# Fused attention and two MLPs on one core: a set's seventh product is transposed later, and other weights are streamed

## The chip, the cores and the metric

One core of a Trainium2 chip runs the whole program. The metric is the device time of one execution in microseconds (us); lower is better. Three runs of the kernel before gave 1410.61, 1415.06 and 1415.53 us, a median of 1415.06.

## What is computed

Everything is float32. With B = 8 batches, 8 heads, 576 queries of 64 and 32 packed queries `p`:

```python
p_packed = softmax_attention(p, k, v)             # 32 rows per head
x = softmax_attention(q, p_packed, p_packed)      # -> [4608, 512]
g = x @ w_gate
x = (g * sigmoid(g) * (x @ w_val)) @ w_out        # 512 -> 1536 -> 512
h = x @ w_in                                      # 512 -> 2048
out = (h * cos(h)) @ w_out2                       # 2048 -> 512
```

The change lies in the last product, `(h * cos(h)) @ w_out2`, called the down phase of the second MLP here.

## The kernel before

The stages follow one another on the TensorE (PE): attention together with the first MLP's up products, the first MLP's down products, the second MLP's up phase (chunks of rows, eight feature pairs each, `period`), and its down phase, which is the loop at L1265. Every float32 operand is split into a high and a low part (`split`, L115: ScalarE (ACT) copies the high part at L116, VectorE (DVE) subtracts it at L117), and three TensorE passes replace one product.

**The down phase.** The 4608 rows are worked in NCH = 5 sets of 2 x 512 rows (the last two of 2 x 384; `TD`). A set's 2 x 2 x 2 block product is done with seven products instead of eight, in the order ORDER = (0, 4, 6, 1, 2, 3, 5); here they are called the first to the seventh product of a set. One product (`down_mm`, L1062) is 48 matmuls: four pairs of feature blocks `fp`, two blocks in each, two halves `m`, three passes. Its left operand is eight weight tiles `wd[n, f]` of 128 x 512 float32 (256 KB), its right operand four split tiles `g2[n, fp]`, called splits here, which `prep2` (L1102) makes from `raw2`, loaded from the scratch tensor `h2` by `load_g` (L1090). Some `raw2` are first replaced by differences (`sums2`, L1109; the subtraction is L1122). The splits have eight buffers (tile name `xs`, L730), enough for two products.

**What comes out.** `evict2` (L1138) is called after a product. After the first, fourth, fifth and sixth product ACT copies the accumulators (L1032) into `part` tiles; after the second, fifth and sixth DVE adds (L1035). `finish_out` (L1124) writes one quarter of a set's output: two DVE transposes (L1128) into a tile `ot`, then four stores (L1133) of 128 KB (96 KB in the small sets). They are queued on POOL (GpSimd), in the last set on SP and ACT. `ot` has two buffers (L1126), so a `finish_out` waits for the four stores of the last but one. The second product finishes one quarter, the sixth finishes two, one behind the other, and the seventh finishes one: its transposes read the accumulators `pb` and `pd` in PSUM directly.

**The weights.** All 56 weight tiles of a set would be needed again in every set. 43 slots of 256 KB exist (`U_AREAS`, L48), handed out in the order in which they were given back (`ut`, L925, `ut_done`, L929). Eight are kept for `part` tiles. Three products' tiles stay for good (24 slots); the four products in `RING` (L51) are streamed, 11 tiles ahead: when a streamed product has been issued, its eight tiles are given back and eight loads (`load_wd`, L960) are issued on SP. The first 35 loads (`wd_first`, L954) are issued late in the up phase, as its weights are given back.

**The order of the work** is written by hand and is the program's order on each engine. For a set `s_` and place `i` it is: the product; `sums2` and the splits of the next product (splits first at the second and fifth product); `load_g` of the next set's rows (at the fifth, sixth and seventh product); the eight weight loads; `evict2`. So SP issues row loads, weight loads and, in the last set, stores in one queue, and DVE meets the seventh product's transposes after the splits of the next set's first product and ahead of those of its second:

```python
                for fp in range(4):
                    if s_ + i:
                        prep2(*nxt2(s_, i), fp)
```

Of the kernel before, what the change touches and what calls it, by code (L numbers as in the profile page):

```python
# [33 lines left out]
NCH = len(TW)  # L34
T0 = tuple(2 * sum(TW[:c]) for c in range(NCH))
D0 = tuple(2 * sum(TD[:c]) for c in range(NCH))
NPF = NF2 // 2
# [10 lines left out]
U_AREAS = (6, 4, 4, 6, 6, 6, 2, 4, 4, 1)  # L48
U_FIRST = (0, 7, 4, 5, 2, 8, 9, 3, 6, 1)
QS = 5  # L50
RING = (4, 1, 3, 5)  # L51
ATT1 = (7, 10, 10, 11, 13, 13, 14, 15, 15, 18, 18, 19, 20)
VISIT1 = (17, 18)
FIRST2 = (14, 14, 14, 16)
# [17 lines left out]
def attention_mlp_kernel(ctx: ExitStack, tc: tile.TileContext, qT, kT, vP, pP, wgv, w12, out):  # L72
# [665 lines left out]
    with tc.manual_schedule():  # L738
# [186 lines left out]
        def ut(key, shape, dt, name):  # L925
            tag_of[key] = free_u.pop(0)
            return lt(shape, dt, "u%d" % tag_of[key], name, U_AREAS[tag_of[key]])

        def ut_done(key):  # L929
            free_u.append(tag_of.pop(key))  # L930
# [20 lines left out]

        wd = {}
        wd_ring = [(n, f) for n in RING for f in range(NPF)] * NCH
        wd_first = [(n, f) for n in (0, 4, 6, 1, 2) for f in range(NPF) if n not in RING]  # L954
        ahead = sum(U_AREAS) - 8 - len(wd_first)
        for k, (n, f) in enumerate(wd_ring[:ahead]):
            wd_first.insert((8 if n == 4 else 16) + k, (n, f))
        del wd_ring[:ahead]

        def load_wd():  # L960
            n, f = (wd_first or wd_ring).pop(0)
            wd[n, f] = ut(("wd", n, f), [128, 2, 256], F32R, "wd")
            SP.dma_start(out=wd[n, f].bitcast(F32).rearrange("p x c -> p (x c)"), in_=w2d[f, PIECE[n]])
# [67 lines left out]
        def copy(out, in_):  # L1031
            ACT.activation(out=out, in_=in_, func=AF.Copy)  # L1032

        def plus(out, x, y):
            DVE.tensor_tensor(out=out, in0=x, in1=y, op=ALU.add)  # L1035
# [26 lines left out]
        def down_mm(s_, i, fps, ms_all=((0, 1),)):  # L1062
            n, w = ORDER[i], TD[s_]
            which = {0: 0, 1: 0, 3: 0, 4: 1, 6: 2, 2: 3, 5: 3}[n]
            first = n in (0, 4, 6, 2)
            if first and 0 in fps:
                if which == 3:
                    acc2[which] = [x[:, :w] for x in bd_tiles()]
                else:
                    o2 = ac_tile("o2")  # L1070
                    acc2[which] = [o2[:, m, :w] for m in range(2)]
            acc = acc2[which]
            for ms in ms_all:
                for fp in fps:
                    for j in range(2):
                        for m in ms:
                            for q, (x, y) in enumerate(PASSES):
                                PE.matmul(  # L1078
                                    out=acc[m], lhsT=wd[n, 2 * fp + j][:, x, 128 * m:128 * m + 128],
                                    rhs=g2[n, fp][:, y, j, :],  # L1080
                                    start=(first and fp + j + q == 0), stop=(fp, j, q) == (3, 1, 2),
                                    skip_group_check=not first,
                                )
            for fp in fps:
                del g2[n, fp]
            return acc
# [3 lines left out]
        def load_g(s_, k, t):  # L1090
            if s_ < NCH:
                w = TD[s_]
                r0 = D0[s_] + w * t
                for fp in range(4):
                    r = raw2[s_, k, t, fp] = xt("raw2", w)
                    f0 = NPF * k + 2 * fp
                    SP.dma_start(out=r, in_=h2[f0:f0 + 2, :, r0:r0 + w].rearrange("f p n -> p f n"))
# [4 lines left out]
        def prep2(s_, n, fp):  # L1102
            if s_ >= NCH:
                return
            r = raw2[(s_, *QUAD[n], fp)]
            g = g2[n, fp] = new_xs(TD[s_])
            split(r, g[:, 0], g[:, 1])

        def sums2(s_, i):  # L1109
            todo = {  # L1110
                1: [((0, 1), (0, 1), (0, 0), fp) for fp in range(4)],
                2: [((1, 1), (1, 1), (0, 1), fp) for fp in range(4)],
                3: [((0, 0), (1, 1), (0, 0), fp) for fp in range(4)],
                4: [((1, 0), (1, 0), (1, 1), fp) for fp in (0, 1)],
                5: [((1, 0), (1, 0), (1, 1), fp) for fp in (2, 3)],
            }
            if s_ == 0:
                todo[1] = [x[fp] for fp in range(4) for x in (todo[1], todo[2])]
                todo[2] = []
            for to, x, y, fp in todo.get(i, ()):  # L1120
                to, x, y = (raw2[(s_, *kt_, fp)] for kt_ in (to, x, y))
                DVE.tensor_tensor(out=to, in0=x, in1=y, op=ALU.subtract)  # L1122

        def finish_out(s_, a, t, o_):  # L1124
            w = TD[s_]
            ot = lt([128, w // 32, 2, 32], F32, "v", "ot", 2)  # L1126
            for m in range(2):
                DVE.transpose(out=ot[:, :, m, :], in_=o_[m])  # L1128
            r0 = D0[s_] + w * t
            queues = (nc.gpsimd,) if s_ < NCH - 1 else (SP, ACT) if (a, t) == (1, 0) else (SP,)  # L1130
            for al in range(4):
                c0 = 128 * al + 64 * a
                queues[al % len(queues)].dma_start(  # L1133
                    out=out[r0:r0 + w, c0:c0 + 64].rearrange("(b r) d -> r b d", r=32),
                    in_=ot[32 * al:32 * al + 32].rearrange("p b m c -> p b (m c)"),
                )

        def evict2(s_, n, acc):  # L1138
            for m in range(2):
                if n in (0, 1, 2, 3):  # L1140
                    part2[n, m] = ut((n, m), [128, TX], F32, "part")[:, :TD[s_]]
                    copy(part2[n, m], acc[m])

            def pop(k):
                for m in range(2):
                    ut_done((k, m))
                return [part2.pop((k, m)) for m in range(2)]

            def add(o_, x, y):
                for m in range(2):  # L1150
                    plus(o_[m], x[m], y[m])

            if n == 2:
                add(acc, pop(1), acc)
            elif n == 4:
                o_ = pop(0)
                add(o_, o_, acc)
                finish_out(s_, 0, 0, o_)
            elif n == 3:
                w_, c22 = pop(3), pop(2)  # L1160
                add(c22, w_, c22)
                finish_out(s_, 1, 1, c22)
                add(w_, w_, acc2[2])
                finish_out(s_, 0, 1, w_)
            elif n == 5:
                finish_out(s_, 1, 0, acc)
# [95 lines left out]
        def nxt2(s_, i):  # L1262
            return (s_, ORDER[i + 1]) if i < 6 else (s_ + 1, ORDER[0])

        for s_ in range(NCH):  # L1265
            for i in range(7):
                n = ORDER[i]
                acc = down_mm(
                    s_, i, (2, 3) if s_ == i == 0 else range(4), ((0,), (1,)) if (s_, i) == (NCH - 1, 6) else ((0, 1),)
                )  # L1270
                if i not in (1, 4):
                    sums2(s_, i)
# [3 lines that stand above are left out]
                if i in (1, 4):  # L1276
                    sums2(s_, i)
                if i == 4:
                    load_g(s_ + 1, 0, 0)
                elif i == 5:  # L1280
                    load_g(s_ + 1, 1, 1)
                    load_g(s_ + 1, 0, 1)
                elif i == 6:
                    load_g(s_ + 1, 1, 0)
                if n in RING:
                    for f in range(NPF):
                        del wd[n, f]
                        ut_done(("wd", n, f))
                        if wd_ring:
                            load_wd()  # L1290
                if s_ or i != 1:
                    if s_ == 0 and i == 2:
                        evict2(s_, *early)
                    evict2(s_, n, acc)
                else:
                    early = n, acc
# [41 lines left out]
```

## Time and profile before

| | us |
|---|---|
| median of three runs (lowest, highest) | 1415.06 (1410.61, 1415.53) |
| the profiled execution | 1411.97 |
| its span, first to last instruction | 1410.2 |
| PE busy in it | 1384.7 |
| VectorE busy | 1121.2 |
| ScalarE busy | 817.6 |
| POOL busy | 239.1 |

The profile is of one execution; its times run from its first instruction. A wait is the idle time of an engine in front of an instruction, with what ended it. PEclk is the granted TensorE clock as a share of its full speed. The down phase takes about the last 365 us of the span.

### The profile page before, as it was taken

The page shows a single profiled execution, that of the slowest core. Times are in us where ns is not written, and L with a number is a line of the kernel's source. Part 1 is how long each engine was busy: PE and PEld are TensorE (multiplying, and loading weights), DVE is VectorE, ACT ScalarE, POOL GpSimd, SP SyncE. Part 2 cuts the span into 40 slices and gives each one's busy share as a digit, 9 for nine tenths or more (in the row PEclk, how much of TensorE's full clock was granted, in tenths as well). Part 3 has the DMA queues.
Part 4 walks back from the last instruction along what each step waited for, and adds up shares of the span by engine and source line. Part 5 has one row for each costly group of instructions (what it writes and reads, how often), then busy time and mean ns, then how long its engine had stood idle before and what let it go on. Part 6 is the DMA issues. An engine that isn't in the chain of part 4 may idle for free.

```text
span 1410.2 us, 23890 instructions
## 1 busy us (share of the span) xinstructions
PE 1384.7 (98%) x8972; PEld 1193.9 (85%) x8972; DVE 1121.2 (80%) x1396; ACT 817.6 (58%) x1119; POOL 239.1 (17%) x392
## 2 busy tenths in 40 slices
PE   8999999999999999999999999999999989999998
PEld 6678888888898888898888999888888878788998
DVE  5779889889866898988857787878679677685876
ACT  5866566666644556554557787768674425253433
POOL 1112222222231111121011111111110010111120
PEclk9999999999999999999999999999999999999999
DMA  8947978877698648458467584748977947657773
GB/s 318 402 178 275 352 260 309 310 283 287 247 410 312 230 163 297 147 193 303 163 263 243 194 290 184 277 147 301 399 273 255 372 129 274 235 178 271 237 269 93
DMA packets 161043, 363.87 MB, mean 258 GB/s; under 512 B 22944, under 2 KB 37792, under 8 KB 159520
## 3 DMA queue, kind: packets, MB, share of 16 engines
q1 hardware_dynamic: 123808, 236.56, 48.5%
q0 software_dynamic: 35456, 123.76, 22.4%
q10 hardware_dynamic: 1664, 2.03, 0.4%
q8 instruction: 71, 1.16, 0.3%
q14 instruction: 44, 0.36, 0.1%
HBM read 236.98 MB, written 125.30 MB: 257 GB/s over the span
## 4 chain that ended last, share of the span: by engine, by line
PE 80%; DMA 7%; issue 6%; DVE 5%; ACT 1%; POOL 1%; SPq 0%; DVEq 0%; POOLq 0%; ACTq 0%
PE o L657 17%; PE ac L992 14%; PE o L1078 13%; PE pv L540 7%; PE pd L992 7%; PE pg L540 7%; PE pb L992 3%; PE wp L500 3%; PE pb L1078 2%; PE pd L1078 2%; PE pv L529 2%; DMA wd<-w2d 1%; PE pg L529 1%; DMA w2u<-w2p 1%; DMA out<-ot 1%
## 5 line engine op out<-in xcount | busy, mean ns | idle before, releaser
L1078 PE MATMUL o<-xs,wd 128*128 128x512 f32 (+1 forms) x1200 | 253.5, 372 | 8.9 <-DVE xs L117 8.9
L657 PE MATMUL o<-g,w 128*128 128x512 f32 (+1 forms) x1260 | 259.7, 368 | 1.4 <-DVE g L117 1.4
L1078 PEld LDWEIGHTS o<-xs,wd 128*128 128x128 f32 x1200 | 221.5, 190 | 39.1 <-DVE xs L117 10.4
L657 PEld LDWEIGHTS o<-g,w 128*128 128x128 f32 x1260 | 219.3, 189 | 41.5 <-DVE g L117 1.9
L992 PE MATMUL ac<-xs,up 128*128 128x512 f32 (+1 forms) x960 | 210.8, 367 | 0.7 <-ACT v L1032 0.7
L992 PEld LDWEIGHTS ac<-xs,up 128*128 128x128 f32 x960 | 175.1, 188 | 23.6 <-ACT v L1032 1.1
L116 ACT ACTIVATE xs<-raw 128x1024 fp32r<-128x1024 f32 (+1 forms) x140 | 130.5, 973 | 98.2 <-DVE raw L1122 77.9
L117 DVE TENSOR_TENSOR xs<-raw,xs 128x1024 fp32r<-128x1024 f32 (+1 forms) x140 | 146.9, 1110 | 12.3 <-ACT xs L116 12.3
L540 PE MATMUL pv<-a,wp 128*128 128x288 f32 x1008 | 150.6, 298 | 3.0 <-DVE h L572 2.8
L540 PEld LDWEIGHTS pg<-a,wp 128*128 128x128 f32 x1008 | 137.7, 188 | 16.8 <-issue 5.7
L116 ACT ACTIVATE g<-hr 128x1024 fp32r<-128x1024 f32 (+1 forms) x105 | 101.3, 976 | 85.7 <-DVE hr L637 35.1
L540 PE MATMUL pg<-a,wp 128*128 128x288 f32 x1008 | 150.3, 298 | 0.4 <-ACT E L213 0.4
L540 PEld LDWEIGHTS pv<-a,wp 128*128 128x128 f32 x1008 | 137.6, 188 | 11.5 <-DVE h L572 5.7
L117 DVE TENSOR_TENSOR g<-hr,g 128x1024 fp32r<-128x1024 f32 (+1 forms) x105 | 113.1, 1114 | 30.0 <-ACT g L116 29.9
L558 ACT ACTIVATE silu<-pg 128x576 f32<-128x576 f32 x96 | 62.5, 652 | 112.7 <-PE pg L540 103.9
L572 DVE TENSOR_TENSOR h<-silu,pv 128x576 f32<-128x576 f32 x96 | 72.1, 751 | 52.2 <-PE pv L540 18.2
L992 PE MATMUL pd<-xs,up 128*128 128x512 f32 (+1 forms) x480 | 111.7, 367 | 0.0
L992 PEld LDWEIGHTS pd<-xs,up 128*128 128x128 f32 x480 | 87.7, 188 | 11.5
L573 POOL DMA_DIRECT2D h<-h x96 | 53.4, 557 | 244.6 <-DVE h L572 222.9
L1133 POOL DMA_DIRECT2D out<-ot x64 | 41.5, 648 | 261.0 <-issue 128.8
L1122 DVE TENSOR_TENSOR raw<-raw,raw 128x1024 f32<-128x1024 f32 (+1 forms) x80 | 84.5, 1109 | 0.1
L1021 DVE SCALAR_TENSOR_TENSOR cp<-ac,cp 128x1024 f32<-128x1024 f32 (+1 forms) x40 | 44.7, 1117 | 46.4 <-ACT cp L1018 42.6
(132 smaller groups left out, 2005.4 us busy)
## 6 DMA issues: line engine op xcount, KB each, us to landing
wd<-w2d SPq DMA_DIRECT2D x184, 256.0 KB, 5.5
up<-w2u SPq DMA_DIRECT2D x140, 256.0 KB, 4.2
h<-h POOLq DMA_DIRECT2D x96, 288.0 KB, 5.4
hr<-h SPq DMA_DIRECT2D x48, 512.0 KB, 7.0
raw<-h SPq DMA_DIRECT2D x48, 512.0 KB, 5.6
raw<-in_w SPq DMA_DIRECT2D x44, 512.0 KB, 4.9
w2u<-w2p POOLq DMA_DIRECT2D x24, 512.0 KB, 4.9
w2d<-w2p POOLq DMA_DIRECT2D x24, 512.0 KB, 5.8
```

Of the source, the lines that this page charges most:

```text
L116: ACT.activation(out=hi, in_=src, func=AF.Copy)
L117: eng.tensor_tensor(out=lo, in0=src, in1=hi.bitcast(F32), op=ALU.subtract)
L500: PE.matmul(out=p_[cols(c), r, :], lhsT=pp_of(b, r, c), rhs=wg[m][rows(r), c // 2, c % 2].rearrange("p a n -> p (a n)"), start=True, stop= ...
L540: PE.matmul(out=p_[:, c, :HS], lhsT=w[:, u, x, o:o + 128], rhs=a2[b][:, u, y, HS * c:HS * c + HS], start=(n == 0), stop=(n == 5),)
L558: ACT.activation(out=s_, in_=pg[:, :, :HS], func=AF.Silu)
L572: DVE.tensor_tensor(out=h_, in0=s_, in1=pv[:, :, :HS], op=ALU.mult)
L573: nc.gpsimd.dma_start(out=h1[f, :, S * b:S * b + S], in_=h_.rearrange("p c n -> p (c n)"))
L657: PE.matmul(out=acc[:, m, :N], lhsT=wd1[n, fp][:, j, 256 * x + 128 * m:256 * x + 128 * m + 128], rhs=g1[n, fp][:, y, j, :], start=(first a ...
L992: PE.matmul(out=out, lhsT=w[:, u, 128 * k:128 * k + 128], rhs=x[:, v, k, :], start=(first and k == 0 and i == 0), stop=(k == 1 and i == 2) ...
L1021: DVE.scalar_tensor_tensor(out=out, in0=h_, scalar=1.0 / TWO_PI, in1=out.bitcast(I32), op0=ALU.mult, op1=ALU.subtract)
L1078: PE.matmul(out=acc[m], lhsT=wd[n, 2 * fp + j][:, x, 128 * m:128 * m + 128], rhs=g2[n, fp][:, y, j, :], start=(first and fp + j + q == 0), ...
L1122: DVE.tensor_tensor(out=to, in0=x, in1=y, op=ALU.subtract)
```

## The change

The streamed products become those at the second to fifth place (numbers 4, 6, 1, 2); the tiles of the first, sixth and seventh (0, 3, 5) stay. The first 35 loads are the eight of product 0, eleven of the ring (eight of 4, three of 6), then those of 3 and 5. And for all sets but the last, `evict2` of the seventh product is called in the next set, after the splits of that set's second product have been issued and just before `evict2` of its first product.

```diff
-RING = (4, 1, 3, 5)
+RING = (4, 6, 1, 2)
...
         wd_ring = [(n, f) for n in RING for f in range(NPF)] * NCH
-        wd_first = [(n, f) for n in (0, 4, 6, 1, 2) for f in range(NPF) if n not in RING]
-        ahead = sum(U_AREAS) - 8 - len(wd_first)
-        for k, (n, f) in enumerate(wd_ring[:ahead]):
-            wd_first.insert((8 if n == 4 else 16) + k, (n, f))
+        ahead = sum(U_AREAS) - 8 - 8 * (7 - len(RING))
+        wd_first = [(0, f) for f in range(NPF)] + wd_ring[:ahead] + [(n, f) for n in (3, 5) for f in range(NPF)]
         del wd_ring[:ahead]
...
                         if wd_ring:
                             load_wd()
-                if s_ or i != 1:
+                if i == 0 and s_:
+                    evict2(*last)
+                if i == 6 and s_ + 1 < NCH:
+                    last = s_, n, acc
+                elif s_ or i != 1:
                     if s_ == 0 and i == 2:
                         evict2(s_, *early)
                     evict2(s_, n, acc)
```

## Rows read from the trace of the kernel before

**Rows 1.** The page, busy time by engine: us, share of the span, instructions.

```profile
PE 1384.7 (98%) x8972; PEld 1193.9 (85%) x8972; DVE 1121.2 (80%) x1396; ACT 817.6 (58%) x1119; POOL 239.1 (17%) x392
```

**Rows 2.** Waits of PE, whole span: who, for whom, us in total, times, longest.

```profile
PE o L1078 <- DVE xs L117: 8.9, 4, 3.9
```

**Rows 3.** Timeline of PE at four set boundaries: start, us, what [idle before, releaser].

```profile
1137.64 2.93 PE L1078 MATMUL o<-xs,wd 128*128 128x512 f32 x6 [3.88 <-DVE xs L117]
...
1217.98 2.37 PE L1078 MATMUL o<-xs,wd 128*128 128x512 f32 x9 [1.50 <-DVE xs L117]
...
1294.95 2.45 PE L1078 MATMUL o<-xs,wd 128*128 128x384 f32 x10 [3.06 <-DVE xs L117]
...
1355.53 2.72 PE L1078 MATMUL o<-xs,wd 128*128 128x384 f32 x14 [0.50 <-DVE xs L117]
```

**Rows 4.** Timeline of DVE at the first boundary.

```profile
1117.26 4.59 DVE L117 TENSOR_TENSOR xs<-raw,xs 128x1024 fp32r<-128x1024 f32 x4
1135.17 0.72 DVE L1128 STREAM_TRANSPOSE ot<-pb 128x512 f32<-128x512 f32 x1 [13.32 <-DMA out<-ot]
...
1136.40 9.13 DVE L117 TENSOR_TENSOR xs<-raw,xs 128x1024 fp32r<-128x1024 f32 x8
```

**Rows 5.** Waits of DVE from 1060 to 1410 us.

```profile
DVE ot L1128 <- DMA out<-ot: 44.9, 5, 13.3
```

**Rows 6.** Timeline of POOL at the first boundary: first and last of eight stores.

```profile
1115.35 0.65 POOL L1133 DMA_DIRECT2D out<-ot  x1 [21.54 <-DVE ot L1128]
...
1143.84 0.66 POOL L1133 DMA_DIRECT2D out<-ot  x1 [2.48 <-issue]
```

**Rows 7.** The out stores issued on POOL from 1115 to 1127 us, three.

```profile
DMA to landing us min/median/max: 5.2/5.4/5.8
```

**Rows 8.** The out stores issued on POOL from 1132 to 1138.1 us, three.

```profile
DMA to landing us min/median/max: 2.4/2.4/2.4
```

**Rows 9.** Stretches: engines' busy us, then PEclk, DMA share, GB/s.

```profile
1117.00:1127.00 10.00, 10.00 (x45) 8.28 (x45) 4.85 (x5) 4.25 (x4) 0.71 (x2) 1.00 1.05 402
1127.00:1135.00 8.00, 6.76 (x30) 5.26 (x28) 0.00 (x0) 1.43 (x3) 1.26 (x2) 1.00 0.42 151
```

**Rows 10.** Stretches behind two of the waits (PEclk is third from the end).

```profile
1137.60:1141.00 3.40, 3.36 (x8) 2.69 (x9) 3.40 (x4) 0.84 (x1) 0.96 (x2) 0.50 0.16 41
...
1295.00:1298.00 3.00, 3.00 (x13) 3.00 (x14) 3.00 (x4) 0.55 (x1) 0.66 (x1) 0.72 0.38 93
```

**Rows 11.** Chain that ended last, pieces: start us, us, what.

```profile
1059.87 30.15 PE o L1078 x133
...
1137.64 35.09 PE o L1078 x143
...
1217.98 32.75 PE o L1078 x143
...
1294.95 26.63 PE o L1078 x143
...
1355.53 25.08 PE o L1078 x143
```

**Rows 12.** Timeline of ACT at the first boundary: first product evicted.

```profile
1133.57 1.09 ACT L1032 ACTIVATE part<-o 128x512 f32<-128x512 f32 x2 [9.82 <-PE o L1078]
```

**Rows 13.** The POOL store issued at 1143.84 us alone.

```profile
DMA to landing us min/median/max: 3.7/3.7/3.7
```

**Rows 14.** Timeline of POOL, third boundary: the eighth store after the sixth product.

```profile
1301.56 0.66 POOL L1133 DMA_DIRECT2D out<-ot  x1 [2.57 <-issue]
```

**Rows 15.** Timeline of SP: first set's last row loads, first ring loads; last set's ring loads.

```profile
1042.60 25.00 SPq L1097 DMA_DIRECT2D raw<-h  x8
1067.69 14.99 SPq L963 DMA_DIRECT2D wd<-w2d  x16
...
1369.00 15.08 SPq L963 DMA_DIRECT2D wd<-w2d  x13
```

**Rows 16.** The weight load issued at 1067.69 us alone.

```profile
DMA to landing us min/median/max: 4.5/4.5/4.5
```

## The prediction, made before the changed kernel ran

> **What bounds the kernel now.** The page comes first: PE is busy 98% of the span [rows 1], so only PE's idle time, or time at a lower clock, can be won. PE's waits: the down phase has one kind, 8.9 us in four, each for a split that DVE writes [rows 2]. Its timeline shows where: in front of the second product of the second to fifth set, 3.88, 1.50, 3.06 and 0.50 us [rows 3], together 8.94.
>
> Why are those splits late? At the first boundary DVE finishes the first product's splits near 1121.9, idles 13.32 us until a store has landed, does the two transposes of the old set's seventh product, then eight splits without a pause [rows 4]: their inputs had long been ready, they only stood behind the transposes. Such waits for stores sum to 44.9 us in five [rows 5]. The transposes need one of two `ot` buffers, so the four stores of the sixth product's first quarter must have landed. POOL issues its stores one after another, the next when the last has landed: 1115.35 is the first, 1143.84 the eighth [rows 6]. The first three took 5.4 us each [rows 7], the next three 2.4 [rows 8]. The DMA share was 1.05 in the first stretch and 0.42 in the second [rows 9].
>
> Two of the waits cost more than their length. After 3.88 us of idling PE runs at the lower of its two levels (granted clock 0.50, so 1.2 instead of 2.4 GHz), and after 3.06 us part of the stretch does (0.72) [rows 10]. The chain prices it: the 143 matmuls that follow (three products) take 35.09 us after the 3.88 us wait and 32.75 after the 1.50 us wait, so 2.34 more; in the small sets 26.63 against 25.08, so 1.55 more [rows 11]. A product thus takes 10.92 us (32.75 / 3), or 8.36 (25.08 / 3).
>
> **The change part by part.** *Transposes moved, four sets.* Eight DVE transposes and sixteen POOL stores go behind the second product's splits. Removed from PE's path: 8.94 + 2.34 + 1.55 = 12.83 us. No instruction is added. On ACT nothing is queued behind them, and POOL has no other work there, so its order stays. `pb` and `pd` stay full until the next set's first product; they are written again only at its fifth, some four products later.
>
> Behind the transposes on DVE now stand the third product's splits. ACT can't copy for these before it has evicted the first product, at 1133.57 [rows 12]; the transposes came free at 1135.17 [rows 4]. The third product would start two products after the first ends, or about 1133.8 + 10.9 = 1144.7, and needs one split of 1.14 us (9.13 / 8). So this place has some 8 us to spare and costs nothing.
>
> *What is late next.* The second product's quarter takes the next `ot` buffer, and so needs the eighth store. If DVE waits there, it holds four subtractions (priced as splits, 4.6 us) and the fourth product's splits. The first product ends at 1137.64 - 3.88 = 1133.76, the fourth starts two products later, at 1155.6; less 1.4 for the transposes (2 x 0.72), 4.6 and 1.14, the eighth store may land as late as 1148.5. It landed at 1143.84 + 3.7 = 1147.5 [rows 6, 13]: 1.0 to spare even at the old pace. At the third boundary, where a small set follows a large one, the first product ends at 1294.95 - 3.06 = 1291.9 and the fourth starts at 1308.6; with the pieces at three quarters (5.4 us together), the limit is 1303.2, and the store of 1301.56 would land at about 1305.3 [rows 14, 13]: 2.1 us late at the old pace, nothing once the stores go 0.3 us each faster.
>
> *Streamed weights.* As many loads as before: 35 first, then 149, 256 KB each. What moves is when. In the old order the sixth and seventh product give back sixteen slots, so weight loads run just when the stores start. In the new one no weight slot comes free between the fifth product and the next set's second; of the eight loads issued after that second product, six have slots free earlier and go with the row loads, the rest wait for PE. So most of the 1.05 share of [rows 9] should be gone and the stores be nearer 2.4 than 5.4 us. By itself this gives the sum nothing; it removes the 2.1. The last row loads of a set no longer stand behind eight weight loads on SP, which only helps.
>
> The price: four streamed products in a row. In steady state each tile is issued over a product ahead of its use, against some 5 us of landing, so nothing shows. Two places are tight. In the first set, tiles four to eight of the third product are issued only after the row loads, which hold SP until about 1067.6; the first ring load goes at 1067.69 [rows 15] and lands 4.5 us later [rows 16], at 1072.2. The fourth product ends at 1059.87 + 30.15 = 1090.0 [rows 11], so the third starts near 1068.2 and wants that tile after 18 of 48 matmuls, at 1072.3. Bounds: 0 late at 4.5 us; 1.2 at the 5.8 us of the slowest loaded store [rows 7]. I take 0.2, since the same queue with the same row loads ahead gave 4.5. In the last set the second product's four stores stand on SP ahead of the fourth product's tiles; ring loads went at 1369.00 [rows 15], 5.1 us after that product's end (1355.53 + 8.36), and the tile is wanted 11.5 us after it (1.375 products): with 4.5 to 5.8 us of landing it has 0.6 to 1.9 to spare.
>
> The Trainium skill has a rule against half of this. SBUF — State Buffer (the "DVE blocks DMA" trap) says that DVE work in certain modes keeps GpSimd from writing the descriptors of its DMAs. By it, moving weight loads would not quicken the stores, and the 2.1 us would stay. The trace speaks against it: DVE did nothing from 1121.9 to 1135.2 [rows 4], and the third store, issued inside that stretch (1115.35 plus two landings), still took over 5 us [rows 6, 7].
>
> *Sum.* 12.83 - 0.2 = 12.6 us; 1411.97 - 12.6 = 1399.4 for the profiled execution, which was 3.1 below the median of the three runs and 1.4 above their lowest. Taken off the median it is 1402.5. I predict between the two, 1401.0.
>
> **The rivals.** *Part of the wait comes back* (0.16). The stores keep their pace, 2.1 us return at the third boundary with up to 1.55 of slow clock, and the first set's tiles are 1.2 late, perhaps with 2.34 of slow clock: at most 7.2 back, so 1403 to 1408. Of this chance 0.06 is for the stores' pace alone, 2.1 to 3.7 us back, 1403.1 to 1404.7. (By the Trainium skill's rule above, that part would come.) For it: both margins are near zero. Against: less DMA traffic at the boundary.
>
> *Nothing gained* (0.08). The second splits would be late for another reason, or the wait reappears whole one product later; about 1414. Against: eight splits without a pause [rows 4], and 8 us to spare behind the transposes.
>
> *Slower* (0.04). The wait for `ot` moves to the second product's quarter and is larger there, since DVE then holds subtractions and splits. With x us from store to store, the eighth lands 8x after the first: in the trace x = (1147.5 - 1115.35) / 8 = 4.0 [rows 6, 13]. The limit there is 1148.5 - 1115.35 = 33.2 us, so from x = 4.15 on each large boundary stalls 8x - 33.2. At x = 5.4, the loaded landing, that is 10.0 us at each of three, with 2.34 of slow clock behind each: 37 lost against 12.8 won, some 1439. It needs the streamed loads, now four products in a row, to fall into the stores. Against: they begin only with the second product.
>
> **How the numbers follow.** A measurement of this kernel can tell about 0.5%, or 7.1 us. The forecast, all four waits and both slow stretches gone, has 0.72: 1397 to 1404 with the spread of the runs shown. The range runs from 1396 to 1407: below, the lowest run less the sum is 1398, with a little for runs whose waits were longer than the profile's; above, it takes in most of the first rival. Faster by over 0.5% is below 1408.0: the forecast and nearly all of the first rival, 0.86. Within 0.5%: 0.10. Slower: 0.04.
>
> **What would show it.** Right: PE's waits for DVE in the down phase under 1 us; no stretch below PEclk 1.00 there but at the end; 143 matmuls behind a boundary in 32.8 (25.1) us; at a boundary DVE does eight splits, then the transposes; the stores after the sixth product land in under 4 us from the second or third on. Wrong: a wait of PE at the fourth product of a set behind `ot` (the slower rival); a wait of PE for a weight load in the first set's third product; a wait of the second splits that remains.

## The result, and the profile after

The changed kernel takes 1398.17 us in the median of four runs (1396.23 to 1401.20), the kernel before 1412.84 in its four; the ratio is 0.9898, with a 95% interval of 0.9868 to 0.9929. The prediction was 1401.0, between 1396 and 1407. The profiled execution took 1396.23 us, with a span of 1394.4.

On the page of the changed kernel (busy us, share and instructions by engine, then the costliest group of the down phase with its idle time at the end), the idle time in front of the down phase's matmuls is gone ([rows 1], [rows 2]).

```profile
PE 1378.6 (99%) x8972; PEld 1190.4 (85%) x8972; DVE 1121.7 (80%) x1396; ACT 817.6 (59%) x1119; POOL 239.1 (17%) x392
...
L1076 PE MATMUL o<-xs,wd 128*128 128x512 f32 (+1 forms) x1200 | 248.4, 367 | 0.0
```

The timelines of DVE and of POOL at the first boundary of the changed kernel (start, us, what, idle before it and releaser):

```profile
1115.57 9.13 DVE L117 TENSOR_TENSOR xs<-raw,xs 128x1024 fp32r<-128x1024 f32 x8
1127.21 0.72 DVE L1126 STREAM_TRANSPOSE ot<-pb 128x512 f32<-128x512 f32 x1 [2.51 <-DMA out<-ot]
...
1133.96 4.63 DVE L117 TENSOR_TENSOR xs<-raw,xs 128x1024 fp32r<-128x1024 f32 x4 [5.43 <-ACT xs L116]
```

```profile
1113.67 0.65 POOL L1131 DMA_DIRECT2D out<-ot  x1 [16.08 <-DVE ot L1126]
1119.00 0.66 POOL L1131 DMA_DIRECT2D out<-ot  x1 [4.68 <-issue]
...
1135.55 0.66 POOL L1131 DMA_DIRECT2D out<-ot  x1 [2.16 <-issue]
```

Against [rows 4], the eight splits of two products now run in one piece ahead of the transposes, and DVE waits 2.51 us for the stores instead of 13.32. Against [rows 6], the eighth store is issued 21.9 us after the first (1135.55 - 1113.67) instead of 28.5. The stretches of [rows 9], at the same times, show why (PEclk, DMA share and GB/s at the end), and so do the six stores after the first, issue to landing:

```profile
1117.00:1127.00 10.00, 10.00 (x46) 8.29 (x45) 7.70 (x7) 2.13 (x2) 1.97 (x3) 1.00 0.45 149
1127.00:1135.00 8.00, 8.00 (x37) 6.64 (x36) 2.36 (x3) 3.11 (x5) 1.97 (x3) 1.00 0.25 65
```

```profile
DMA to landing us min/median/max: 2.4/2.4/2.8
```

The DMA share fell from 1.05 to 0.45 (to 0.57 from 1115.3 to 1125.3 us, which is as far behind the first store as the stretch of [rows 9] was). What SP issued there before (start, us, what):

```profile
1110.95 2.39 SPq L1097 DMA_DIRECT2D raw<-h  x4
1113.63 11.88 SPq L963 DMA_DIRECT2D wd<-w2d  x14
```

Now SP issues four weight loads there, from 1115.1 to 1116.6 us, and nothing else from 1110 to 1133. The first store, beside those four, still took 5.0 us. The chain of the changed kernel has no break at a boundary any more; the first four products of a set are one piece each (192 matmuls):

```profile
1120.97 43.52 PE o L1076 x192
...
1197.13 43.52 PE o L1076 x192
...
1273.29 33.30 PE o L1076 x192
...
1331.56 33.28 PE o L1076 x192
```

Three quarters of 43.52 are 32.64, and of 33.28 they are 24.96: the pace that [rows 11] shows behind the short waits, without the 35.09 and 26.63 behind the long ones.

### The profile page after: what moved, and what is told of

The parts are those of the page before. It is cut to its first block, busy times and chain, and to the rows that moved or that the text cites. A ratio compares the mean times of both kernels' runs of the same rounds, so it can differ in the third digit from the quotient of the medians.

```text
span 1394.4 us, 23883 instructions
## 1 busy us (share of the span) xinstructions
PE 1378.6 (99%) x8972; PEld 1190.4 (85%) x8972; DVE 1121.7 (80%) x1396; ACT 817.6 (59%) x1119; POOL 239.1 (17%) x392
## 4 chain that ended last, share of the span: by engine, by line
PE 89%; DVE 4%; DMA 3%; issue 2%; ACT 1%; POOL 0%; ACTq 0%; POOLq 0%; SPq 0%; DVEq 0%
PE o L1076 18%; PE o L657 17%; PE ac L990 14%; PE pd L990 7%; PE pv L540 7%; PE pg L540 7%; PE pb L990 4%; PE pd L1076 4%; PE pb L1076 4%; PE wp L500 2%; PE pv L529 2%; PE pg L529 1%; DMA qt<-in_qT 1%; DMA hr<-h 1%; PE tp L229 1%
## 5 line engine op out<-in xcount | busy, mean ns | idle before, releaser
L1076 PE MATMUL o<-xs,wd 128*128 128x512 f32 (+1 forms) x1200 | 248.4, 367 | 0.0
L1076 PEld LDWEIGHTS o<-xs,wd 128*128 128x128 f32 x1200 | 218.5, 188 | 28.1
L1120 DVE TENSOR_TENSOR raw<-raw,raw 128x1024 f32<-128x1024 f32 (+1 forms) x80 | 84.5, 1110 | 0.1
```

The costliest lines, as they stand in the source:

```text
L1076: PE.matmul(out=acc[m], lhsT=wd[n, 2 * fp + j][:, x, 128 * m:128 * m + 128], rhs=g2[n, fp][:, y, j, :], start=(first and fp + j + q == 0), ...
```

## The experiments

Each kernel was timed beside the kernel before on the same chip. The first two make one half of the change each.

**The transposes moved, the weights as before.** The edit is the second half of the diff alone:

```diff
+                if i == 0 and s_:
+                    evict2(*last)
+                if i == 6 and s_ + 1 < NCH:
+                    last = s_, n, acc
+                elif s_ or i != 1:
```

> Only the transposes of the seventh product are moved; the streamed weights are those of before. Theory (the splits were late only because they stood behind the transposes): the four waits of 8.9 us and the slow clock of 3.9 us go even though the stores keep their old pace, 5 to 6 us for the first two or three at a boundary; about 2 us come back as a wait of PE at the fourth product of the fourth set, where the eighth store lands too late for the second product's quarter. Ratio to before 0.991 to 0.993. Rival (the stores' pace is what counts, the order on DVE only shifts the wait): PE's waits for DVE in the down phase stay over 5 us in total, at the third or fourth product, and the ratio is over 0.995.

Measured: ratio 0.9938 (0.9916 to 0.9959). PE's waits in the down phase, then the first three stores at the first boundary, issue to landing:

```profile
PE o L1078 <- DVE xs L117: 2.1, 1, 2.1
PE o L1078 <- ACT xs L116: 1.2, 1, 1.2
```

```profile
DMA to landing us min/median/max: 5.2/5.2/5.3
```

The timeline of DVE at the third boundary shows the place, the second product's quarter:

```profile
1295.12 1.01 DVE L1035 TENSOR_TENSOR part<-part,o 128x384 f32<-128x384 f32 x2
1300.65 1.04 DVE L1128 STREAM_TRANSPOSE ot<-part 128x384 f32<-128x384 f32 x2 [4.52 <-DMA out<-ot]
1301.61 3.52 DVE L1122 TENSOR_TENSOR raw<-raw,raw 128x768 f32<-128x768 f32 x4
1305.05 1.82 DVE L117 TENSOR_TENSOR xs<-raw,xs 128x768 fp32r<-128x768 f32 x2
```

The four waits are gone though the stores are as slow as in [rows 7], and a wait comes back where the limit of the prediction placed it, behind the `ot` buffer of the second product's quarter at the third boundary: 1.2 and 2.1 us in front of the fourth product's first matmuls, 3.3 where about 2 was expected. The rival, that the wait would only shift, is out; the ratio came a little above the expected range, as the 1.2 us and the slow clock behind the wait came on top.

**The weights changed, the transposes as before.** The edit is `RING` and `wd_first` of the diff.

> Only the streamed weights are changed; the transposes stay ahead of the second product's splits. Theory: weight loads no longer run beside the first stores, so after the first one or two a store lands in 2.4 us, the fourth about 13 us after the first was issued instead of 20. The transposes then run some 4 us before the first product ends, the second splits are ready in time, and the waits are under 1 us in total, the clock never drops: ratio 0.990 to 0.993, so that either part alone wins nearly all and the two do not add. Rival (GpSimd's stores are held up by something else than the weight loads, DVE's work for instance): first stores of 5 us as before, waits of 8.9 us as before, ratio 0.998 to 1.002.

Measured: ratio 0.9907 (0.9885 to 0.9929), with no wait of PE for DVE in the down phase. DVE at the first boundary:

```profile
1117.60 4.59 DVE L117 TENSOR_TENSOR xs<-raw,xs 128x1024 fp32r<-128x1024 f32 x4
1128.67 0.72 DVE L1126 STREAM_TRANSPOSE ot<-pb 128x512 f32<-128x512 f32 x1 [6.48 <-DMA out<-ot]
...
1129.91 4.59 DVE L117 TENSOR_TENSOR xs<-raw,xs 128x1024 fp32r<-128x1024 f32 x4
```

DVE still waits in front of the transposes, but 6.48 us instead of 13.32. The first product, 10.9 us from 1123.0, ends at 1133.9; the second splits start 4 us ahead of that. The chain from the start of the first set's fifth product to the start of the last transpose:

```profile
1090.36 0.68 PE pb L1076 x3
...
1391.87 0.58 DVE ot L1126
```

That is 301.51 us, and the changed kernel's chain takes the same 301.51 there (its two lines are shown below). So this half alone wins all that the whole wins, and the halves do not add: each takes away the same waits. The weight loads and the row loads both run earlier in this kernel; which of them counts for how much was not tried.

**The changed kernel again**, beside these.

> The changed kernel unaltered, beside the others on one chip. Both theories: ratio 0.987 to 0.993 as measured before; no wait of PE for DVE in the down phase. It gives the difference of each part to the whole on the same chip.

Measured: ratio 0.9900 (0.9880 to 0.9919), 1399.41 us. PE waited for DVE nowhere in the down phase. The difference to the kernel with the weights alone is inside the intervals.

**The waits filled with matmuls**, in the kernel before:

```diff
+                if s_ and i == 1:
+                    hold = ac_tile("hold")
+                    for _ in range((0, 14, 5, 10, 0)[s_]):
+                        PE.matmul(
+                            out=hold[:, 0], lhsT=wd[0, 0][:, 0, :128], rhs=wd[0, 0].rearrange("p x c -> p (x c)"),
+                            start=True, stop=True,
+                        )
```

> The kernel before, with 14, 5 and 10 additional matmuls into an unused accumulator ahead of the second product of the second, third and fourth set, which fill 3.2, 1.1 and 2.3 us of the waits and compute nothing that is used. Theory (the slow stretch comes from PE's idling): the granted clock stays at full level, the three products behind the first and third wait take 32.8 and 25.1 us instead of 35.1 and 26.6, and 2 to 4 us are saved: ratio 0.997 to 0.9985. Rival (the stretch is slow because DVE delivers splits late behind the transposes): these times stay as they were, or the kernel gets slower, ratio 0.9995 or more.

Measured: ratio 0.9975 (0.9962 to 0.9988). PE at the first boundary, and the chain's pieces behind the four:

```profile
1131.68 3.34 PE L1271 MATMUL hold<-wd 128*128 128x512 f32 x14
1134.85 5.38 PE L1078 MATMUL o<-xs,wd 128*128 128x512 f32 x21
```

```profile
1135.37 32.75 PE o L1078 x143
...
1214.94 32.75 PE o L1078 x143
...
1292.72 25.09 PE o L1078 x143
...
1351.66 25.06 PE o L1078 x143
```

The splits come no earlier than before and the waits are filled in part (PE still idled 1.95 and 1.57 us at the second and third boundary), and 35.09 and 26.63 us became 32.75 and 25.09. PE's idling is what slowed it; that term, 3.9 us by [rows 11], is 3.5 by the ratio (0.0025 of 1412.55), with 1.7 to 5.4 inside the interval.

**The third product's weight tiles earlier in the first set.** In the second profiled execution of the changed kernel PE waited 0.9 us for a weight load there, in the first it had not. So here five tiles are loaded ahead of the last four row loads:

```diff
         load_g(0, 1, 1)
+        for _ in range(5):
+            load_wd()
         load_g(0, 0, 1)
...
-                        if wd_ring:
+                        if wd_ring and (s_, i) != (0, 1) or f > 4 and wd_ring:
```

> The changed kernel, but in the first set the third product's last five weight tiles are loaded ahead of the last four row loads, not after them. Theory (PE waits there in some executions for the fourth tile: the weight load after 1070.25 us came 1.55 us late-to-next in the second look at the changed kernel, against a usual 0.23): no gap there, the chain no longer passes through a weight load or a store of the up phase, 0 to 1.3 us saved against the changed kernel, ratio to before 0.987 to 0.992. Rival (the row loads, now 2.4 us later on SP, become the late ones): a wait of PE for splits in the first set, and the kernel 1 to 4 us slower than the changed one.

> The changed kernel unaltered, beside the others: ratio 0.988 to 0.992; a gap of up to 1.6 us between weight loads near 1070 us, or none.

Measured: 1397.45 us, ratio 0.9895 (0.9873 to 0.9918), against 1400.01 and 0.9911 (0.9891 to 0.9930) for the changed kernel. In the latter's profile PE waited in front of the third product's fourth tile (waits of PE, then its timeline):

```profile
PE o L1076 <- DMA wd<-w2d: 1.4, 1, 1.4
```

```profile
1069.83 3.56 PE L1076 MATMUL o<-xs,wd 128*128 128x512 f32 x15
1074.79 5.51 PE L1076 MATMUL o<-xs,wd 128*128 128x512 f32 x23 [1.40 <-DMA wd<-w2d]
```

In the former it waited for nothing in the down phase. To tell whether it is the faster kernel, both were timed again:

> The kernel with the five early tiles a second time, to tell whether it beats the changed one by more than the spread. Theory (a wait of 1 to 2 us in most executions of the changed kernel goes): median 1 to 2 us below the changed kernel's in the same sitting, no gap between weight loads over 0.35 us in the down phase. Rival (the 2.6 us between the two medians of the sitting before were spread): medians within 1 us of each other, either way.

> The changed kernel unaltered beside it: ratio to before 0.988 to 0.992; in the first set a wait of PE for a weight load of 0 to 1.5 us.

Measured: 1398.82 (0.9905, 0.9885 to 0.9925) and 1399.00 us (0.9909, 0.9890 to 0.9928). Again the wait was 1.4 us in the changed kernel and absent in the other, but the medians now lie 0.2 us apart, so most of the 2.6 us between those of the first pair was spread. The wait is gone in both profiled executions with early tiles, its 1.4 us are less than these runs can tell, and no version is shown to beat the changed kernel.

**Slower stores.** The four stores of the sixth product's first quarter are issued twice in the first four sets, once in the changed kernel and once with the transposes left where they were:

```diff
-            for al in range(4):
+            for al in range(4) if s_ == NCH - 1 or (a, t) != (1, 1) else (0, 0, 1, 1, 2, 2, 3, 3):
```

> The changed kernel with the four stores of the sixth product's first quarter issued twice (the same data), in the first four sets. So the first ot buffer comes free after eight stores and the second after twelve. Theory of the limit (the second quarter's last store may land 33.2 us after the first was issued at a large boundary, about 27 at the third): no wait at the second or third product; 2 to 4 us of wait at the fourth product after the first two boundaries, 8 to 12 after the third, ratio to before 1.000 to 1.006. Rival (nothing on PE waits for stores once the transposes are moved): ratio 0.990 to 0.994.

> The same doubled stores, with the new streamed weights but the transposes left ahead of the second product's splits. Theory (here the limit is nearer: the first quarter's stores must land before the first product ends, about 17 us after the first was issued): 7 to 10 us of wait at the second product of the second, third and fourth set each, with a slow clock behind each, ratio to before 1.008 to 1.018, so the move is worth 8 to 20 us where stores are slower, though next to nothing where they are not. Rival (the move is worth nothing in any case): the same time as with the transposes moved, within 3 us.

Measured: 1431.47 us with the transposes moved, ratio 1.0150 (1.0119 to 1.0180), and 1439.77 without, 1.0196 (1.0174 to 1.0219). So the move is worth 8.3 us here (every run with it is faster than every run without), at the low end of what was expected, and both are slower than expected. PE's waits, moved and not moved:

```profile
PE o L1076 <- DVE xs L117: 13.5, 6, 3.5
PE o L1076 <- ACT xs L116: 7.0, 4, 2.1
```

```profile
PE o L1076 <- DVE xs L117: 32.9, 4, 9.7
```

The expectation for the unmoved one left out the fourth boundary, which waited like the others (7.97 us). For the moved one, "no wait at the second or third product" failed: the third product waited 0.38 us at the first boundary and 3.51 at the third. With the fourth product's waits that makes 5.1, 4.9, 7.7 and 2.8 us at the four boundaries, where 2 to 4, 2 to 4, 8 to 12 and none were expected, and the clock was lower behind each of them (0.50 to 0.72). The first boundary on DVE shows what the limit had missed:

```profile
1141.65 0.72 DVE L1126 STREAM_TRANSPOSE ot<-pb 128x512 f32<-128x512 f32 x1 [16.16 <-issue]
...
1142.89 4.59 DVE L117 TENSOR_TENSOR xs<-raw,xs 128x1024 fp32r<-128x1024 f32 x4
1147.40 4.62 DVE L1120 TENSOR_TENSOR raw<-raw,raw 128x1024 f32<-128x1024 f32 x4
1151.94 1.28 DVE L1033 TENSOR_TENSOR part<-part,o 128x512 f32<-128x512 f32 x2
1153.60 1.31 DVE L1126 STREAM_TRANSPOSE ot<-part 128x512 f32<-128x512 f32 x2 [0.38 <-DMA out<-ot]
1154.83 4.59 DVE L1120 TENSOR_TENSOR raw<-raw,raw 128x1024 f32<-128x1024 f32 x4
1159.34 4.62 DVE L117 TENSOR_TENSOR xs<-raw,xs 128x1024 fp32r<-128x1024 f32 x4
```

The second quarter's store, which the limit was about, held DVE only 0.38 us. It was the seventh product's transposes, late by their own stores, that pushed a row of work almost without gaps: from 1141.65 to the fourth product's splits at 1159.34 it is 17.7 us. (The profile names no releaser for the transposes' 16.16 us; the last of the eight stores ahead of them was issued on POOL at 1137.77 and landed 3.6 us later, at 1141.4.)

## Why the prediction was right, and where its terms were off

**The waits.** That the splits were late only for their place in DVE's queue is shown by the kernel with the move alone: slow stores, and the four waits gone. The term was 8.94 us, and it was too small. From the start of the first set's fifth product to the start of the last transpose, the chain of the kernel before and that of the changed one give

```profile
1090.02 0.68 PE pb L1078 x3
...
1405.62 0.58 DVE ot L1128
```

```profile
1088.33 0.68 PE pb L1076 x3
...
1389.84 0.58 DVE ot L1126
```

315.60 and 301.51 us, 14.1 saved where 12.83 were summed. (The other 1.7 us between the profiled executions lie ahead of that point, where the change moves nothing but the order of some weight loads. In the attention PE waited 1.4 us for a load of `qt` in the profile of before and not in that of the changed kernel; nothing here ties that to the change.) The page of before has a better measure of the waits than [rows 2], the idle time in front of PE's weight loads (last on the line, with its releaser):

```profile
L1078 PEld LDWEIGHTS o<-xs,wd 128*128 128x128 f32 x1200 | 221.5, 190 | 39.1 <-DVE xs L117 10.4
```

10.4 + 3.89 = 14.3, within 0.2 of the 14.1. So PE's idle time tells each of the four waits some 0.37 us too short. One part of that is seen: a matmul's end in the trace is modelled, and a 128x512 matmul is recorded with 394 ns where 227 pass from one to the next (43.52 / 192), so its end lies some 0.17 us behind the point from which the next could have run. The rest is not explained.

**The slow clock.** 3.89 us by the chain. With the waits filled the two pieces shortened by 3.88, and the kernel by 3.5 (1.7 to 5.4). Right.

**The streamed weights.** "By itself this gives the sum nothing" failed. The prediction counted the waits to the move and the 2.1 us at the third boundary to the weights. The mechanism was right, stores of 2.4 us once the weight loads are gone; but the transposes' start under quick stores was not worked out, and it alone clears the second splits with 4 us to spare. In the changed kernel the first transpose starts at 1127.21, ahead of the first product's end near 1131.9, so there the move has nothing left to take. The sum is the same, since both halves take the same waits, and that the number came out although the prediction gave the waits to one half alone is luck. The move alone takes 306.95 us where the whole takes 301.51 (chain, as above): 5.4 short, with the late eighth store at the third boundary that was forecast as 2.1 and measured 3.3 and the lower clock behind it.

On the stores' pace, the Trainium skill's trap in SBUF — State Buffer (the "DVE blocks DMA" trap), that DVE work in certain modes keeps GpSimd from writing descriptors, names copies as such work. That the subtractions and transposes which DVE does here are of that kind was assumed when the prediction made a rival of it, and no run shows it: the stores were quick with the new weights. The trace of before also shows two stores of 2.4 us while DVE was busy throughout (issue to landing of the two, then the stretch; DVE busy is the third number after the length):

```profile
DMA to landing us min/median/max: 2.4/2.4/2.4
```

```profile
1164.00:1169.40 5.40, 5.40 (x26) 4.46 (x25) 5.40 (x6) 3.95 (x4) 1.31 (x2) 1.00 0.25 53
```

**The price of four streamed products in a row.** Bounds of 0 to 1.2 us, 0.2 taken. Four profiled executions of the changed kernel show 0, 0.9, 1.4 and 1.4: the place was right, the size too small, and the upper bound as well. So one of the prediction's signs of being wrong, a wait of PE for a weight load there, did appear, in three of four profiles. It is paid once, and is less than the spread of the runs.

**The spare room behind the transposes.** "Some 8 us to spare" looked only at the next product, and left out the two transposes themselves: they take 1.2 us ([rows 4]: 1135.17 to 1136.40), so it was 7. (The third product starts one product after the first ends, as that sum has it, not two as the sentence says.) The slower stores show that 17.7 us of DVE work, and a split of 1.2, stand between the transposes' start and the fourth product, which begins two products (21.8 us) after the first ends: so they may start about 3 us after that end, not 8. In the kernel before they came free 1.4 us after it ([rows 3], [rows 4]); with the move alone nothing was lost there, so the size did not matter to the result.

**The rivals.** Nothing gained and slower are out, and of the first rival only the late tiles came. The slower rival's place, the second product's quarter, exists (2.1 us with the move alone), but with slower stores the transposes themselves were the first to be late.

## What to carry to other kernels

When an engine with a fixed order of work waits for a transfer, look first at what stands behind the waiting instruction: moving it behind work whose inputs are ready removes the wait without making the transfer faster. Then ask what slows the transfer; if one cure is enough, the two do not add (here the new weights alone won everything, the move alone all but 5.4 us), and the second buys room for worse days (8.3 us with doubled stores) rather than time. Judge that room by all the work queued on the engine up to the next deadline it can miss, not by the next item.

## What the runs showed of the hardware

POOL's stores of 128 KB landed in 2.4 to 2.8 us in stretches with a DMA share of 0.25 to 0.45, and in 5.2 to 5.8 us when issued beside weight and row loads at a share near 1, so there the stores, one in flight at a time, lose more than half their pace. Weight loads alone do it: in the kernel before, the third store, issued at 1126.95, took 5.4 us, though the last row load, issued at 1113.0, had landed 8.3 us after that. Of PE's waits those of 3.88 and 3.06 us were followed by the lower clock, and so, with the move alone, was the pair of 1.2 and 2.1 us with one matmul between them; waits of 1.50 and 1.4 us alone were not, nor was one of 1.95 us with five filling matmuls close ahead of it. The stretches behind the pair and behind the wait of 1.4 us (PEclk third from the end):

```profile
1306.20:1309.20 3.00, 3.00 (x12) 3.00 (x13) 3.00 (x4) 0.00 (x0) 0.66 (x1) 0.64 0.18 44
```

```profile
1074.80:1078.00 3.20, 3.20 (x14) 2.67 (x15) 3.17 (x3) 1.87 (x2) 0.00 (x0) 1.00 1.02 379
```

With doubled stores and the transposes moved, a wait of 3.51 us and four more pairs, from 0.72 and 2.08 to 2.06 and 2.87 us, were followed by a granted clock of 0.50 to 0.72. These are the cases; what else decides it they do not show.
